# Attention with top-1 routed experts: gate weights, scalings, low parts and a tile's turn in another order

## The chip, the cores and the metric

The kernel runs on one core of a Trainium2 chip. The metric is the device time of one execution in microseconds; the time of a kernel is the median of several runs. The core has a matrix engine (TensorE, PE in the rows), VectorE (DVE), ScalarE (ACT), GpSimd (POOL) and SyncE (SP), which here only issues transfers.

## The reference, cut to what matters

Decayed linear attention over blocks gives `x`; each of its 1536 rows is routed to the one expert with the largest logit, up to a capacity, and scaled with its softmax weight.

```python
# attention: B=2, H=8, S=768, D=64, blocks of 64
intra = einsum('bhij,bhjd->bhid', einsum('bhic,bhjc->bhij', qb, kb) * Dmask, vb)
inter = einsum('bhid,bhde->bhie', qb * lam_pow, kv_state)
out[:, :, sl] = intra + inter
kv_state = lam_block * kv_state + einsum('bhsd,bhse->bhde', kb * rev_pow, vb)
# experts: N=1536, D=512, E=8, F=1024, capacity 384
x = out.transpose(0, 2, 1, 3).reshape(B * S, H * D)
logits = x @ w_gate
expert_idx = argmax(logits, axis=1)
gate_w = softmax(logits)[arange(N), expert_idx]
# the first `capacity` rows of each expert, in order
h = maximum(einsum('ecd,edf->ecf', disp, w1), 0.0)
y = einsum('ecf,efd->ecd', h, w2)
out[i] = gate_w[i] * y[expert_idx[i], pos[i]]
```

## The kernel before, in words

The attention works in chunks of 128 rows, twelve in all (`NTILE`), six for each of the two batches (`NC`). The order of every instruction is written out by hand, and each engine takes its own queue strictly in that order. A chunk passes these steps, spread over several iterations `s` of one loop:

- `load` (L262, SyncE): 512 KB of queries and keys (`qk`) and 512 KB of keys and values (`kv`), four buffers each.
- `decay_q` (L406) and `decay_k` (L417), GpSimd: `qd` and `kd`, scaled with powers of the decay; `kp` (L303, ScalarE) holds those for the keys.
- `score` (L438, TensorE) and `mask` (L448, VectorE), two chunks ahead.
- `state(s)` (L497): the update of the running state on TensorE, added on VectorE (L505, L507) to `tmp`, the old state scaled by ScalarE in `carry` (L485, four instructions).
- `attend(s)` (L464, L471): the chunk's output in PSUM, copied by ScalarE to `xT` (L476).
- `turn(s - 1)` (L520): the output is transposed and multiplied with the gate weights, which lie beside the identity in `iw` (L275, four small transfers issued by ScalarE).
- `gate(s - 1)`: VectorE adds up the logits `l` (L526, L530), finds maximum, index and the one-hot row `oh` (L547); ScalarE copies the row to `xg` (L532, L537) and makes `nm`, `ex` and the sum (L551, L554).
- `place(s - 2)` (L576 to L582): TensorE counts the rows of each expert, VectorE (L583, L587) and GpSimd (L591) make the slot. `scatter` (L608, GpSimd) writes the row into its expert's list in memory; `pad` (L128) writes zeros behind the lists, with the row numbers in `padi`.

The `l` sum, the copy of `xg` (L532) and `oh` read one PSUM bank, `lg`.

Weights come in pieces of 512 KB (L96, four buffers `wraw`). Each is split in a high part `whi` on ScalarE (L103) and a low part `wlo` on VectorE (L111). Pieces 0 to 5 are split within the loop: `HI` puts the high part of piece i at the end of iteration 5 + i, `LO` the low part at the end of iteration 6 + i.

Expert 0 is done in two tiles of 128 rows, `first` and `second` (class `Solo`). `turn` transposes the tile's rows (L192), which SyncE loaded (L161), `rest` makes their low part `xl` (L197), `up` multiplies with one weight piece (L210; after an odd piece ScalarE writes `raw`, L215), `cross` transposes back (L220) and splits into `hh` (L222) and `hl` (L223), `down` multiplies with the second weights (L234). During the attention `first` takes its PSUM banks (`x`, `t`, `h`) in turn from the three buffers that `score` uses. Experts 1 to 7 follow in a loop with 256 rows each (L811, L836); their rows are transposed on VectorE in `shuffle` (L726) and split in `trans` (L736, L737).

Of the kernel before, what the change touches and what calls it, by code (L numbers as in the profile page):

```python
# [18 lines left out]
P = 128  # L19
# [3 lines left out]
E, DFF = 8, 1024  # L23
NT = B * S
NC = S // P
NTILE = NT // P
# [15 lines left out]
def kernel(  # L42
# [71 lines left out]
    def split_w(i):  # L114
        split_hi(i)
        split_lo(i)
# [64 lines left out]
    class Solo:  # L181
# [17 lines left out]

        def up(self, p, between=None):  # L200
            if p % 2 == 0:
# [5 lines left out]
            for n, (a, b, k) in enumerate(terms):  # L207
                if between and n == 2:
                    between()
                nc.tensor.matmul(  # L210
                    ps, lhsT=a[:, P * k:P * k + P], rhs=b[:, k], start=(n == 0), stop=(n == 3 * KD - 1)
                )
# [31 lines left out]
    def attention():  # L244
        with ExitStack() as c2:
# [26 lines left out]
            iw = ac.tile([P, KD, P + E], F32, name="iw")  # L272
            for g in range(2):
                for r in range(2):
                    nc.scalar.dma_start(  # L275
                        out=iw[64 * g:64 * g + 64, r::2, P:P + E], in_=wg[64 * r:64 * r + 64, 2 * g:2 * g + 2]
                    )
            for i in range(1, 4):
# [16 lines left out]
            for a in range(HP):  # L295
# [9 lines left out]
                in_=dt[:, :, :, P - 1:P].rearrange("p r a o -> p a r o"), func=AF.Copy,  # L305
            )

            def busy(n, late=False):
# [169 lines left out]
            def carry(s):  # L478
                c = s % NC
                if c == NC - 1 or c == 0:  # L480
                    return
                old = mem[s % 2]
                tmp[s] = p2.tile([P, HP, D], F32, tag="tmp", name="tmp", bufs=1)
                for a in range(HP):
                    nc.scalar.activation(  # L485
                        out=tmp[s][:, a], in_=old[:, a], func=AF.Copy, scale=qp[:, a, P - 1:P]
                    )
# [34 lines left out]
            def gate(s):  # L522
                if s < 0:
                    return
                l = sm.tile([P, E], F32, tag="l", name="l")
# [8 lines left out]
                )  # L534
                if s == NTILE - 2:
                    first.turn()
                nc.scalar.activation(  # L537
                    out=xg[:, 0:KD - 1],
                    in_=tpp[s][:, :, 0:P].rearrange("p k (g d) -> p k g d", g=2), func=AF.Copy,
                )  # L540
                m8 = sm.tile([P, 8], F32, tag="m8", name="m8")
                nc.vector.max(out=m8, in_=l)
# [64 lines left out]
            def scatter(s):  # L607
# [4 lines left out]
                apart(i, "xs", s >= EARLY)  # L612

            decay_k(0)
            for a in range(HP):
# [9 lines left out]
            load(5, 0)  # L625
            tokens()
            mask(1)
            for s in range(NTILE):
                decay_k(s + 1)
                if s > 0:  # L630
                    state(s, (0, 1, 2, 3))
                attend(s)
                carry(s + 1)
                for k in range(KD):
                    turn(s - 1, k)
                gate(s - 1)
                place(s - 2)
                if s == NTILE - 1:
                    first.rest()
                    for k in range(KD):  # L640
                        turn(s, k)
                    place(s - 1)
# [3 lines left out]
                weight(s - 1)  # L646
                if s in LO:
                    split_lo(LO[s])
                if s in HI:
# [23 lines left out]
            gate(s)  # L673
            first.up(0)
            split_hi(6)
# [27 lines left out]
    def ffn(first):  # L703
        with ExitStack() as c2:
# [62 lines left out]
            second.up(0)  # L767
            shuffle(1, 0)
            shuffle(1, 1)
            second.up(1)  # L770
            split_w(10)
            load_w(14)
            second.up(2)
            second.cross(0)
            split_w(11)
            load_w(15)
# [284 lines left out]
```

## Time and profile before

| | us |
|---|---|
| median of 3 runs | 258.04 (257.35 to 260.33) |
| the profiled execution, its own time | 257.75 |
| its span | 256.0 |
| TensorE busy in it | 237.9 (93%) |
| VectorE, ScalarE, GpSimd busy | 158.0, 132.9, 81.1 |

The span runs from the first to the last instruction; 1.75 us of the profiled time lie outside of it. In rows of a timeline the first number is the start, the second the duration, both in us; the bracket at the end tells how long the engine stood idle before it and what released it. Transposes of the expert rows and the first tile lie between 57 and 93 us, the loop over experts 1 to 7 behind that.

### The profile page before, as it was taken

How to read it: one execution, taken by the hardware profiler on the slowest of the kernel's cores; microseconds unless marked ns; L12 is line 12 of the kernel's file. 1: busy time of each engine (PE TensorE's matmuls, PEld its weight loads, DVE VectorE, ACT ScalarE, POOL GpSimd, SP SyncE). 2: the span in 40 equal slices, each digit the busy share in tenths (PEclk: the TensorE clock that was granted, in tenths of full speed). 3: DMA queues.
4: the chain of work that ended last, by engine and by line, in shares of the span. 5: the costliest groups of instructions: out<-in, count | busy, mean ns of one | idle time of the engine just before them, and what ended most of it. 6: DMA issues, size and time to landing. Idle time of an engine off the chain costs nothing.

```text
span 256.0 us, 5405 instructions
## 1 busy us (share of the span) xinstructions
PE 237.9 (93%) x2071; PEld 211.2 (83%) x2071; DVE 158.0 (62%) x335; ACT 132.9 (52%) x240; POOL 81.1 (32%) x100
## 2 busy tenths in 40 slices
PE   7989999789899899999999999999999999999950
PEld 3778888678778689889989988998998898899850
DVE  4756577788772786792793778479276757912100
ACT  2154556866662685664673656457446546622110
POOL 4583559896585120006004101400500210030130
PEclk9999999999999999999999999999999999999995
DMA  5998899947759869966688497789749698210010
GB/s 131 408 403 301 243 330 386 407 163 249 220 179 276 262 214 316 279 247 250 185 295 264 141 302 237 227 226 308 257 106 319 230 249 242 84 73 3 1 64 3
DMA packets 26894, 58.14 MB, mean 227 GB/s; under 512 B 6377, under 2 KB 13547, under 8 KB 26864
## 3 DMA queue, kind: packets, MB, share of 16 engines
q1 hardware_dynamic: 22752, 50.36, 61.7%
q0 software_dynamic: 3536, 7.37, 7.6%
q8 instruction: 18, 0.29, 0.5%
q10 hardware_dynamic: 576, 0.02, 0.1%
q14 instruction: 12, 0.10, 0.1%
HBM read 50.37 MB, written 11.56 MB: 242 GB/s over the span
## 4 chain that ended last, share of the span: by engine, by line
issue 58%; POOL 15%; PE 10%; DMA 6%; DVE 6%; ACT 1%; POOLq 1%; SPq 0%; DVEq 0%
POOL xs L128 7%; POOL out L175 5%; DMA wraw<-in_wp 4%; PE sc L438 2%; DVE wlo L111 2%; DMA qk<-in_qkv 2%; PE x L464 2%; PE tp L520 2%; PE st L497 1%; PE x L471 1%; DVE pt L448 1%; POOL qd L406 1%; POOL kd L417 1%; POOL out L874 1%; PE solo_ps L210 1%
## 5 line engine op out<-in xcount | busy, mean ns | idle before, releaser
L111 DVE TENSOR_TENSOR wlo<-wraw,whi 128x1024 fp32r<-128x1024 f32 x64 | 77.2, 1216 | 10.9 <-ACT whi L103 8.1
L103 ACT ACTIVATE whi<-wraw 128x1024 fp32r<-128x1024 f32 x64 | 66.6, 1051 | 10.2 <-DMA wraw<-in_wp 10.2
L811 PE MATMUL h<-xh,whi 128*128 128x256 f32 x224 | 61.9, 276 | 0.0
L811 PE MATMUL h<-xl,whi 128*128 128x256 f32 x224 | 61.9, 276 | 0.0
L811 PE MATMUL h<-xh,wlo 128*128 128x256 f32 x224 | 61.9, 276 | 0.0
L175 POOL DMA_INDIRECT out<-y,ti x13 | 13.3, 1025 | 123.7 <-ACT y L844 123.4
L819 DVE SCALAR_TENSOR_TENSOR hl<-h,hh 128x512 fp32r<-128x512 f32 x28 | 19.4, 692 | 40.5 <-ACT hh L818 40.5
L811 PEld LDWEIGHTS h<-xl,whi 128*128 128x128 f32 x224 | 42.1, 188 | 0.3
L811 PEld LDWEIGHTS h<-xh,whi 128*128 128x128 f32 x224 | 42.0, 188 | 0.3
L811 PEld LDWEIGHTS h<-xh,wlo 128*128 128x128 f32 x224 | 42.1, 188 | 0.0
L836 PE MATMUL y<-whi,hl 128*128 128x512 f32 x104 | 41.0, 394 | 0.0
L836 PE MATMUL y<-wlo,hh 128*128 128x512 f32 x104 | 40.8, 392 | 0.0
L836 PE MATMUL y<-whi,hh 128*128 128x512 f32 x104 | 40.4, 388 | 0.0
L818 ACT ACTIVATE hh<-h 128x512 fp32r<-128x512 f32 x28 | 16.8, 598 | 41.0 <-PE h L811 41.0
L836 PEld LDWEIGHTS y<-wlo,hh 128*128 128x128 f32 x104 | 19.5, 188 | 4.3
L836 PEld LDWEIGHTS y<-whi,hh 128*128 128x128 f32 x104 | 19.5, 188 | 4.1
L836 PEld LDWEIGHTS y<-whi,hl 128*128 128x128 f32 x104 | 19.6, 188 | 3.9
L128 POOL DMA_INDIRECT xs<-zero,padi x16 | 18.3, 1142 | 4.9 <-issue 4.6
L476 ACT ACTIVATE xT<-x 128x512 f32<-128x512 f32 x12 | 7.1, 592 | 20.2 <-PE x L471 12.5
L608 POOL DMA_INDIRECT xs<-xg,slot x12 | 15.8, 1313 | 3.7 <-POOL slot L591 1.1
L448 DVE TENSOR_TENSOR pt<-sc,dt 128x512 f32<-128x512 f32 (+1 forms) x26 | 15.6, 643 | 1.9 <-PE sc L438 1.4
L844 ACT ACTIVATE y<-y,wt 128x512 f32<-128x512 f32 x13 | 8.9, 687 | 13.2 <-PE y L836 12.5
(133 smaller groups left out, 355.5 us busy)
## 6 DMA issues: line engine op xcount, KB each, us to landing
wraw<-in_wp SPq DMA_DIRECT2D x64, 512.0 KB
qk<-in_qkv SPq DMA_DIRECT2D x12, 512.0 KB
kv<-in_qkv SPq DMA_DIRECT2D x12, 512.0 KB
rw<-xs SPq DMA_DIRECT2D x28, 128.0 KB
rw<-xs SPq DMA_DIRECT2D x2, 257.0 KB
xs<-zero,padi POOLq DMA_INDIRECT x16
out<-y,ti POOLq DMA_INDIRECT x13
xs<-xg,slot POOLq DMA_INDIRECT x12
```

What stands on the lines that cost most here:

```text
L103: nc.scalar.activation(out=hi, in_=raw[i], func=AF.Copy)
L111: nc.vector.tensor_tensor(out=lo, in0=t, in1=hi.bitcast(F32), op=ALU.subtract)
L128: i = nc.gpsimd.indirect_dma_start(out=xs, out_offset=bass.IndirectOffsetOnAxis(ap=padi[:, e, t:t + 1], axis=0), in_=zero, in_offset=None, ...
L175: i = nc.gpsimd.indirect_dma_start(out=out, out_offset=bass.IndirectOffsetOnAxis(ap=ti[e][:, t:t + 1], axis=0), in_=y, in_offset=None, bou ...
L448: nc.vector.tensor_tensor(out=pt[s][:, r, a], in0=sc[s][r][:, a], in1=dt[:, r, a], op=ALU.mult)
L476: nc.scalar.activation(out=xT[s], in_=x[:, :, 0:2 * P], func=AF.Copy)
L608: i = nc.gpsimd.indirect_dma_start(out=xs, out_offset=bass.IndirectOffsetOnAxis(ap=slot[:, s:s + 1], axis=0), in_=xg_all[:, s], in_offset= ...
L811: nc.tensor.matmul(ps[:, f], lhsT=a[:, k, fs], rhs=b[:, k], start=(n == 0), stop=(n == 3 * KD - 1),)
L818: nc.scalar.activation(out=hh, in_=ps, func=AF.Relu)
L819: nc.vector.scalar_tensor_tensor(out=hl, in0=ps, scalar=0.0, in1=hh.bitcast(F32), op0=ALU.max, op1=ALU.subtract)
L836: nc.tensor.matmul(yp[t], lhsT=a[:, f, tsl], rhs=b[:, f], start=(p == 0 and f == 0 and n == 0), stop=(p == 3 and f == 1 and n == 2),)
L844: nc.scalar.activation(out=y, in_=yp[t], func=AF.Copy, scale=wt[e][:, t, 0:1])
```

## The change

The four transfers of the gate weights are issued behind the copy `kp`. `tokens()`, seven small GpSimd instructions that make row numbers, stands ahead of the first `decay_k`. `carry` of the next chunk is called within `gate`, behind the copies of `xg`, instead of behind `attend`. The low part of a weight piece is made right behind `state` instead of at the end of the same iteration. The first tile's `turn` moves from the gate of chunk 10 to that of chunk 9, its `rest` to the end of iteration 10, and its `up(0)` into iteration 11, with the last chunk's turn after its fifth matmul and the placement of chunk 10 behind it. The two `shuffle` calls of expert 1 move behind `second.cross(0)`.

```diff
--- before.py
+++ after.py
@@ -197,7 +197,7 @@
             nc.vector.tensor_tensor(out=self.xl, in0=self.xp, in1=self.xh.bitcast(F32), op=ALU.subtract)
             tokens_of(0, self.t)
 
-        def up(self, p, between=None):
+        def up(self, p, between=None, at=2):
             if p % 2 == 0:
                 self.hn[p // 2] = self.ps("h")
             ps = self.hn[p // 2][:, 256 * (p % 2):256 * (p % 2) + 256]
@@ -205,7 +205,7 @@
             terms = [(self.xh, w, k) for k in range(KD) for w in (wh, wl)]
             terms += [(self.xl, wh, k) for k in range(KD)]
             for n, (a, b, k) in enumerate(terms):
-                if between and n == 2:
+                if between and n == at:
                     between()
                 nc.tensor.matmul(
                     ps, lhsT=a[:, P * k:P * k + P], rhs=b[:, k], start=(n == 0), stop=(n == 3 * KD - 1)
@@ -270,11 +270,6 @@
             load(0, 0)
             load(0, 1)
             iw = ac.tile([P, KD, P + E], F32, name="iw")
-            for g in range(2):
-                for r in range(2):
-                    nc.scalar.dma_start(
-                        out=iw[64 * g:64 * g + 64, r::2, P:P + E], in_=wg[64 * r:64 * r + 64, 2 * g:2 * g + 2]
-                    )
             for i in range(1, 4):
                 load(i, 0)
                 load(i, 1)
@@ -304,6 +299,11 @@
                 out=kp.rearrange("p (a r) o -> p a r o", r=2),
                 in_=dt[:, :, :, P - 1:P].rearrange("p r a o -> p a r o"), func=AF.Copy,
             )
+            for g in range(2):
+                for r in range(2):
+                    nc.scalar.dma_start(
+                        out=iw[64 * g:64 * g + 64, r::2, P:P + E], in_=wg[64 * r:64 * r + 64, 2 * g:2 * g + 2]
+                    )
 
             def busy(n, late=False):
 
@@ -477,7 +477,7 @@
 
             def carry(s):
                 c = s % NC
-                if c == NC - 1 or c == 0:
+                if c == NC - 1 or c == 0 or s >= NTILE:
                     return
                 old = mem[s % 2]
                 tmp[s] = p2.tile([P, HP, D], F32, tag="tmp", name="tmp", bufs=1)
@@ -521,6 +521,7 @@
 
             def gate(s):
                 if s < 0:
+                    carry(s + 2)
                     return
                 l = sm.tile([P, E], F32, tag="l", name="l")
                 nc.vector.tensor_reduce(
@@ -532,12 +533,13 @@
                 nc.scalar.activation(
                     out=xg[:, KD - 1], in_=lgp[s][:, 0:P].rearrange("p (g d) -> p g d", g=2), func=AF.Copy
                 )
-                if s == NTILE - 2:
-                    first.turn()
                 nc.scalar.activation(
                     out=xg[:, 0:KD - 1],
                     in_=tpp[s][:, :, 0:P].rearrange("p k (g d) -> p k g d", g=2), func=AF.Copy,
                 )
+                if s == NTILE - 3:
+                    first.turn()
+                carry(s + 2)
                 m8 = sm.tile([P, 8], F32, tag="m8", name="m8")
                 nc.vector.max(out=m8, in_=l)
                 i8 = sm.tile([P, 8], U32, tag="i8", name="i8")
@@ -611,6 +613,7 @@
                 )
                 apart(i, "xs", s >= EARLY)
 
+            tokens()
             decay_k(0)
             for a in range(HP):
                 score(0, a)
@@ -623,29 +626,27 @@
             for a in range(HP):
                 score(1, a)
             load(5, 0)
-            tokens()
             mask(1)
             for s in range(NTILE):
                 decay_k(s + 1)
                 if s > 0:
                     state(s, (0, 1, 2, 3))
+                if s in LO:
+                    split_lo(LO[s])
                 attend(s)
-                carry(s + 1)
                 for k in range(KD):
                     turn(s - 1, k)
                 gate(s - 1)
                 place(s - 2)
+                if s == NTILE - 2:
+                    first.rest()
                 if s == NTILE - 1:
-                    first.rest()
-                    for k in range(KD):
-                        turn(s, k)
+                    first.up(0, lambda: [turn(s, k) for k in range(KD)], 5)
                     place(s - 1)
                 for a in range(HP):
                     score(s + 2, a)
                 mask(s + 2)
                 weight(s - 1)
-                if s in LO:
-                    split_lo(LO[s])
                 if s in HI:
                     split_hi(HI[s])
                 load(s + 4, 1)
@@ -671,7 +672,6 @@
                 nc.vector.reduce_max(out=cmax, in_=ct, axis=mybir.AxisListType.X)
 
             gate(s)
-            first.up(0)
             split_hi(6)
             first.up(1, lambda: place(s))
             weight(s)
@@ -765,13 +765,13 @@
             first.finish()
             second.rest()
             second.up(0)
-            shuffle(1, 0)
-            shuffle(1, 1)
             second.up(1)
             split_w(10)
             load_w(14)
             second.up(2)
             second.cross(0)
+            shuffle(1, 0)
+            shuffle(1, 1)
             split_w(11)
             load_w(15)
             second.up(3)
```

## Rows read from the trace of the kernel before

**Rows 1.** The page's first line, then windows: us, each engine's busy time, clock, DMA share, GB/s.

```profile
span 256.0 us, 5405 instructions
...
6.50:93.50 87.00, 79.90 (x1026) 68.94 (x1027) 60.27 (x216) 49.73 (x133) 53.48 (x60) 1.00 0.84 290
93.50:242.00 148.50, 148.50 (x992) 135.69 (x991) 94.51 (x111) 80.64 (x103) 21.53 (x21) 1.00 0.68 213
```

**Rows 2.** TensorE's waits, 6 to 94 us: waited for, us in total, times, longest.

```profile
PE st L497 <- issue: 1.8, 2, 1.1
PE st L497 <- POOL kd L417: 1.3, 2, 1.0
PE solo_ps L234 <- DVE solo_hl L223: 1.0, 1, 1.0
PE st L576 <- DVE mem L507: 0.8, 1, 0.8
...
PE solo_ps L210 <- DVE solo_xl L197: 0.4, 1, 0.4
```

**Rows 3.** Timeline of GpSimd: start, us, engine, line, operation, tiles, count.

```profile
11.38 0.17 POOL L385 IOTA padi<- 128x16 int32 x1
...
13.04 1.04 POOL L417 TENSOR_TENSOR kd<-kv,kp 128x512 f32<-128x512 f32 x1
```

**Rows 4.** Waits of SyncE's queue, 0 to 94 us; timelines of ScalarE and TensorE.

```profile
SPq L262 <- DMA iw<-in_wg: 4.7, 4, 2.1
...
6.50 0.21 ACT L303 ACTIVATE kp<-dt 128x8 f32<-128x8 f32 x1 [1.48 <-DVE dt L297]
...
16.27 0.96 PE L520 MATMUL tp<-iw,xT 128*128 128x136 f32 x6
```

**Rows 5.** Timeline around the gate of chunk 2; brackets: idle before, releaser.

```profile
26.51 1.05 ACT L485 ACTIVATE tmp<-mem,qp 128x64 f32<-128x64 f32 x4
...
27.75 0.17 DVE L547 TENSOR_TENSOR oh<-lg,i 128x8 f16<-128x8 f32 x1 [0.63 <-ACT xg L532]
```

**Rows 6.** Timeline of ScalarE and VectorE around the gate of chunk 6.

```profile
43.19 1.06 ACT L103 ACTIVATE whi<-wraw 128x1024 fp32r<-128x1024 f32 x1 [2.26 <-DMA wraw<-in_wp]
...
45.88 0.17 DVE L547 TENSOR_TENSOR oh<-lg,i 128x8 f16<-128x8 f32 x1 [1.16 <-ACT xg L532]
```

**Rows 7.** Timeline of VectorE and ScalarE, an early iteration and one low part.

```profile
17.27 0.18 DVE L526 TENSOR_REDUCE l<-tp 128x8 f32<-128x24 f32 x1 [1.92 <-PE tp L520]
...
18.83 0.18 ACT L554 ACTIVATION_READ_ACCUMULATOR ex<-l,nm 128x1 f32 x1
...
21.63 0.18 DVE L526 TENSOR_REDUCE l<-tp 128x8 f32<-128x24 f32 x1 [1.17 <-PE tp L520]
...
47.58 1.21 DVE L111 TENSOR_TENSOR wlo<-wraw,whi 128x1024 fp32r<-128x1024 f32 x1
```

**Rows 8.** Timeline around the first tile, and the loads of both tiles' rows.

```profile
57.20 0.33 SPq L161 DMA_DIRECT2D rw<-xs  x1
...
67.81 0.17 PE L576 MATMUL st<-oh,upper 128*128 128x8 f16 x1 [0.66 <-DVE oh L547]
...
68.25 1.04 ACT L103 ACTIVATE whi<-wraw 128x1024 fp32r<-128x1024 f32 x1
...
69.37 0.60 ACT L215 ACTIVATE solo_raw<-solo_ps 128x512 f32<-128x512 f32 x1
...
74.73 0.33 SPq L161 DMA_DIRECT2D rw<-xs  x1
...
78.12 0.63 PE L192 MATMUL solo_ps<-ident,rw 128*128 128x128 f32 x4 [0.24 <-DMA rw<-xs]
```

**Rows 9.** Timeline of VectorE and ScalarE in the second tile.

```profile
84.79 1.30 DVE L726 STREAM_TRANSPOSE xf<-rw 128x512 f32<-128x512 f32 x2
...
85.50 0.60 ACT L222 ACTIVATE solo_hh<-solo_ps 128x512 fp32r<-128x512 f32 x1 [1.05 <-PE solo_ps L220]
...
87.12 0.68 DVE L223 TENSOR_TENSOR solo_hl<-solo_ps,solo_hh 128x512 fp32r<-128x512 f32 x1
```

## The prediction

> **What bounds the kernel now.** I read the windows view first, because it says which stages can give anything at all. From 93.5 to 242 us TensorE is busy 148.50 of 148.50 us [rows 1]. The reader is to see a stage with no hole: whatever happens before 93.5 moves its start, and nothing else in it can be won by reordering the other engines. From 6.5 to 93.5 it is busy 79.90 of 87.00, so it stands still for 7.1 us [rows 1]. All of the change lies there, so 7.1 us is the ceiling of what removed waits can bring. Next I read TensorE's waits in that stretch, which say whom it waits for: `st` for issue or for the decayed keys `kd` (3.1 together), the second tile's `hl` (1.0), the running state `mem` (0.8), the first tile's `xl` (0.4) [rows 2]. No engine is full there; the waits are matters of order in queues that each run strictly in order. So I read the timelines around each wait, and for each moved instruction I ask what now stands behind it.
>
> The sum is made against the profiled execution's own time: span 256.0 [rows 1] and 1.75 around it, 257.75. That is 0.3 below the median of 258.04. All gains below are in us, plus is faster.
>
> **The change part by part.**
>
> *Token numbers first.* The seven small instructions of `tokens()` start at 11.38 and hold GpSimd until `kd` of chunk 1 starts at 13.04: 1.66 us [rows 3]. In their new place GpSimd only waits for the first loads. TensorE's longest wait for `kd` is 1.0 [rows 2], and it is this one. After the move `kd` would start 1.6 sooner, more than the 1.0 that is asked. Gain 1.0; less if the third chunk's load is late next, more if the gap lets the following iteration start early. I keep 0.7 to 1.3.
>
> *Gate weights later.* Their four issues stand first on ScalarE's queue, and SyncE stands still 4.7 us in four waits for them while it has chunk loads to send [rows 4]. Sent behind the `kp` copy of 6.50 [rows 4], they no longer share with the first loads. The bound below is 0 (the later loads pay instead); the bound above is about 0.6, as only the first two loads hold TensorE up. I take 0.4. Behind the four issues on ScalarE nothing is due before the first `xT`. Their first user is the gate of chunk 0, at 16.27 [rows 4], some 1.4 sooner after the change, at 14.9; the deadline has to hold or the part is lost (a rival below).
>
> What speaks against this part stands in the Trainium skill, "DMA: Bandwidth & Descriptors", section "Queues, rings and completion order": each DMA engine takes turns between the queues it has work for, packet by packet. By it the small gate transfers share with the big loads whenever they are sent, and the cost only moves to later loads; this part would bring 0, and the sum would be 0.4 lower. The rows cannot decide it, since SyncE's waits [rows 4] show issues held back and not packets.
>
> Prologue together: 1.0 + 0.4 = **+1.4**.
>
> *State scalings behind the copies.* `oh` waits for ScalarE's `xg` copy, 0.63 at 27.75, because four `tmp` scalings of 1.05 together stand ahead of it [rows 5]. One of the two `st` waits under "issue" (1.8 in two) is the 1.1 of chunk 8, where `oh` waited 1.16 [rows 2, 6]; the rest, 0.7, belongs to this place in the early chunks, and I take **+0.6** there. Price: `tmp` now stands ahead of `nm`, `ex` and the accumulated sum, which come 1.0 later. Two things hang on them: the row weight on VectorE, and `whi` on ScalarE.
>
> *Low parts behind the state update.* Removed with it, in iterations 6 to 10: 1.1 (`st`, chunk 8), 0.8 (`mem`) and the 0.3 that is left of `kd` [rows 2], together 2.2. What is late next: `wlo` of one piece now follows `whi` of that piece directly, and ahead of the gate's `l`. That closes a loop: from `l` to the end of the accumulated sum is 18.83 + 0.18 - 17.27 = 1.74, then `tmp` 1.05 [rows 5], `whi` 1.06 [rows 6], `wlo` 1.21, then the next `l` [rows 7]. The raw sum is 5.06; neighbours on an engine overlap by about 0.1 each, which leaves some 4.76. An iteration without weight work takes 21.63 - 17.27 = 4.36 [rows 7]. So the loop and not TensorE would set the pace, 0.4 more per iteration, and six iterations (6 to 11) have a low part: 6 x 0.4 = 2.4 given back. Bounds: 0 if GpSimd and VectorE have slack enough for the loop not to close (the low part may lie in the shadow of `attend`), 3.0 if neighbours do not overlap. Net **-0.2**, from +2.2 to -0.8.
>
> *First tile a chunk sooner.* Removed: the wait for `xl`, 0.4 [rows 2]. Added: (1) the last but one placement now stands behind the whole of `up(0)`, and the last gate's `l` behind that placement's VectorE work and `weight`. The wait for the last `oh` is 0.66 now [rows 8]. Counted from the end of the last turn, TensorE wants it after the seven matmuls that are left of `up(0)`, the placement and two matmuls, about 1.2; `oh` is there after the placement (1.0), its VectorE work with `weight` (0.7) and the seven small operations from `l` to `oh` (1.1), about 2.8, an estimate from durations near 0.17 [rows 5, 7]. The wait becomes 1.6: -0.9. (2) PSUM's three banks rotate, and one allocation moved: `up(2)` gets the bank of the first hidden half, which is free only when ScalarE's `raw` has read it. `raw` starts at 69.37, behind `whi` at 68.25 (1.04) [rows 8]; `up(2)` follows the gate closely, so about 0.7 of wait is new (0 if the low-part work in front shrinks, 1.1 if all of `whi` counts). (3) The tile's rows are asked for at 57.20; the second tile's took from 74.73 to 78.12, 3.4 us, with TensorE waiting [rows 8]. The turn now falls near 60, so 57.2 + 3.4 = 60.6 may be up to 0.5 late; the rest moves with the same chain, and I take 0. Together **-1.2**, from -2.0 to +0.4.
>
> *Stream transposes behind `cross(0)`.* `hl` starts at 87.12 only because two transposes (1.30) and a low part stood before it; `hh` was done at 85.50 + 0.60 = 86.10 [rows 9]. So `hl` comes 1.0 sooner, and the 1.0 that TensorE waited [rows 2] goes. But the transposes, `wlo` and the expert's `xl` now queue ahead of the second `hl`, which TensorE wants early as well: 86.8 + 1.3 + 1.2 + 0.7 = 90.0, then 0.7 for itself, 90.7, wanted at about 90.2. 0.5 comes back. **+0.5**, from 0 to 1.0.
>
> Sum: 1.4 + 0.6 - 0.2 - 1.2 + 0.5 = +1.1, so 257.75 - 1.1 = 256.65, near **256.7**.
>
> **The rivals.**
>
> *A, removed waits stay removed.* If the low part lies wholly in the shadow of `attend`, the 2.4 of the loop are not paid, and if the bank of `up(2)` is free in time the 0.7 is not either: 1.1 + 2.4 + 0.7 = 4.2 gain, 253.5. For it: VectorE and ScalarE are far from full, 60.27 and 49.73 of 87 [rows 1]. Against it: the loop's five steps are each in the rows, and none of them is optional.
>
> *B, the weight piece lands no sooner (the other side).* Piece 1 makes `whi` wait until 43.19, 2.26 us for its load [rows 6]. So far only its low part waited with it; now that low part stands ahead of the gate of chunk 6. If the piece comes at the same time in spite of an earlier chain, `wlo` ends 43.19 + 1.06 + 1.21 = 45.46, and eight small VectorE operations of about 0.17, such as `l` and `oh` [rows 5, 7], later `st` of chunk 8 can start, at 46.85. Before it started 0.42 behind the `oh` of 45.88 [rows 6], at 46.30. All that was gained until there is lost and 0.55 more; behind it remain +1.1 of waits, -1.2 (three rounds of the loop), -1.2 and +0.5: -1.35, so 259.1. It decides if the piece lands less than about 1.3 sooner than now. Against it: SyncE's issue of the piece hangs on the same chunks, which come sooner.
>
> *C, gate weights late.* If they land after 14.9, TensorE waits in the gate of chunk 0. Issued behind `kp` they have 14.9 - 6.7 = 8 us, in which full chunk loads stand ahead of them; SyncE's longest single wait for them, 2.1 [rows 4], speaks for less. The prologue's 1.4 would go: 258.1.
>
> **How the numbers follow.** Forecast 0.53 (its own range 255.4 to 258.2: the errors of the loop, the bank and the prologue against each other), A 0.20, B 0.11, C 0.09, other 0.07. The range 254.0 to 259.2 takes in B and the nearer half of A and leaves out about 2 in 10. About 1% is what a measurement can tell from no change here: 255.46 and 260.6. Faster needs 2.3 off: A and the low end of the forecast, 0.25. Slower needs B with another mishap, 0.06. The rest, 0.69, lies within 1%.
>
> **What would show it.** Prologue: no wait for `kd` before `st` of chunk 1, SyncE without waits for `iw`, no wait of the first gate matmuls for `iw`. Loop: in iterations 7 to 10 `l` directly behind `wlo`, and `wlo` behind `whi`; the time from one `l` to the next near 4.76. A: it would be 4.4 there and no wait of TensorE. B: `wlo` of piece 1 idle for `whi`, and that for its load, near 43. First tile: `up(2)` waiting for `raw`, and `place` of chunk 11 for `oh` over 1 us. Second tile: no wait at the first `hl`, about 0.5 at the second. The start of expert 1 should move from 93.5 by the sum, to about 92.4. I am wrong if the loop does not close, if the rows or the gate weights are late, or if expert 1 itself gets holes.

## The result, and the profile after

The changed kernel is slower: 261.1 us median of 20 runs against 258.3 of the kernel before in the same comparison, ratio 1.0104 with an interval of 1.0071 to 1.0137. The forecast was 256.7. All ratios leave out executions more than 1.5% above the fastest of their kernel; the profiled one of the changed kernel is such an execution, but later profiles that are not show the same low parts of 2.6 us. The profiled execution of the changed kernel took 263.73, above its own median; its expert loop ran at 22.31 us per expert where another execution of the same kernel ran at 21.89 (first experiment below), so in what follows the two traces are compared by the places that lie ahead of that loop, above all by the start of expert 1 and by the starts of `st`, the state update of a chunk.

The page's first line and the windows view of the kernel after (columns as in [rows 1]):

```profile
span 262.0 us, 5412 instructions
...
6.50:93.50 87.00, 77.93 (x1021) 67.59 (x1022) 62.40 (x213) 49.31 (x133) 48.81 (x53) 1.00 0.82 288
93.50:100.00 6.50, 6.50 (x53) 6.29 (x52) 5.42 (x6) 4.22 (x5) 1.24 (x1) 1.00 0.79 252
```

In the stretch in which TensorE stood still for 7.1 us before [rows 1] it now stands still for 9.1, and behind it there is again no hole. TensorE's waits of the kernel after, 6 to 100 us:

```profile
PE st L497 <- POOL slot L593: 1.9, 1, 1.9
PE st L497 <- issue: 1.6, 1, 1.6
PE st L497 <- POOL kd L417: 1.6, 3, 0.9
PE st L578 <- DVE oh L549: 1.2, 1, 1.2
PE solo_ps L234 <- DVE solo_hl L223: 1.0, 1, 1.0
PE sc L438 <- DMA qk<-in_qkv: 0.7, 1, 0.7
PE solo_ps L192 <- DMA rw<-xs: 0.6, 1, 0.6
PE solo_ps L234 <- ACT solo_hh L222: 0.6, 1, 0.6
```

Against [rows 2] the reader is to see that the waits for `mem` and `xl` are gone as forecast, and that larger ones stand in front of `st`: 1.6 and 1.9 instead of 1.1 and 0.4. Where the time went, by the starts of TensorE's rows in the two timelines:

| place | before | after | gained so far |
|---|---|---|---|
| `st` of chunk 1 | 14.13 | 13.12 | +1.01 |
| `st` of chunk 6 | 36.71 | 35.20 | +1.51 |
| `st` of chunk 8 | 46.30 | 45.62 | +0.68 |
| `st` of chunk 9 | 51.19 | 52.06 | -0.87 |
| `st` of chunk 10 | 56.95 | 57.46 | -0.51 |
| second tile's turn | 78.12 | 78.55 | -0.43 |
| expert 1 | 93.47 | 94.52 | -1.05 |

Two places lose: chunks 7 to 9, over 2 us, and the second tile, 0.6. The first is the larger, and this is its timeline (GpSimd, VectorE and TensorE of the kernel after):

```profile
36.93 1.22 DVE L111 TENSOR_TENSOR wlo<-wraw,whi 128x1024 fp32r<-128x1024 f32 x1
...
37.82 1.23 POOL L417 TENSOR_TENSOR kd<-kv,kp 128x512 f32<-128x512 f32 x1
...
41.05 1.04 POOL L610 DMA_INDIRECT xs<-xg,slot  x1 [0.15 <-POOL qd L406]
...
41.64 2.62 DVE L111 TENSOR_TENSOR wlo<-wraw,whi 128x1024 fp32r<-128x1024 f32 x1 [0.28 <-ACT whi L103]
...
42.12 1.05 POOL L417 TENSOR_TENSOR kd<-kv,kp 128x512 f32<-128x512 f32 x1
...
44.19 0.17 DVE L527 TENSOR_REDUCE l<-tp 128x8 f32<-128x24 f32 x1
...
45.62 0.69 PE L497 MATMUL st<-kv,kd 128*64 128x64 f32 x16 [1.64 <-issue]
...
47.75 2.62 DVE L111 TENSOR_TENSOR wlo<-wraw,whi 128x1024 fp32r<-128x1024 f32 x1 [0.28 <-ACT whi L103]
...
48.23 1.05 POOL L417 TENSOR_TENSOR kd<-kv,kp 128x512 f32<-128x512 f32 x1
```

The low part that took 1.20 to 1.23 in the kernel before (1.21 in [rows 7]) takes 2.62, twice. Both times `kd` lies inside it, at its usual 1.05, and the low part ends 1.09 behind the end of `kd` (42.12 + 1.05 = 43.17, and 41.64 + 2.62 = 44.26). At 36.93 the low part begins 0.89 ahead of `kd`; there it keeps its time and `kd` is the one that grows, to 1.23. The explanation that the experiments test, there called Theory P: a low part and a `kd` don't read at the same time, one stands until the other is done. The Trainium skill, "SBUF — State Buffer", section "Who interferes with whom", has this rule: a VectorE instruction with two inputs in SBUF contends with a GpSimd instruction that reads SBUF, and the one that was issued second stands until the other is done. The trace agrees that it is all or nothing (2.62, with the end 1.09 behind that of `kd`); that the low part, begun 0.48 ahead, was the one to wait is not what the rule says.

### The profile page after: what moved, and what is told of

It is laid out like the page before. It is cut to its first block, busy times and chain, and to the rows that moved or that the text cites. A ratio compares the mean times of both kernels' runs of the same rounds, so it can differ in the third digit from the quotient of the medians.

```text
span 262.0 us, 5412 instructions
## 1 busy us (share of the span) xinstructions
PE 240.1 (92%) x2071; PEld 213.7 (82%) x2071; DVE 161.2 (62%) x335; ACT 133.5 (51%) x240; POOL 77.8 (30%) x100
## 2 busy tenths in 40 slices
DMA packets 26896, 58.15 MB, mean 222 GB/s; under 512 B 6378, under 2 KB 13548, under 8 KB 26865
## 4 chain that ended last, share of the span: by engine, by line
issue 58%; PE 14%; POOL 12%; DVE 6%; DMA 2%; ACT 2%; POOLq 1%; SPq 0%; DVEq 0%
POOL xs L128 6%; POOL out L175 5%; DVE wlo L111 3%; PE x L464 3%; PE sc L438 3%; PE tp L520 3%; DMA kv<-in_qkv 2%; PE x L471 2%; PE st L497 2%; PE solo_ps L210 1%; POOL kd L417 1%; DVE pt L448 1%; ACT whi L103 1%; ACT tmp L485 1%; PE lg L520 1%
## 5 line engine op out<-in xcount | busy, mean ns | idle before, releaser
L111 DVE TENSOR_TENSOR wlo<-wraw,whi 128x1024 fp32r<-128x1024 f32 x64 | 80.1, 1262 | 16.3 <-ACT whi L103 16.3
L811 PE MATMUL h<-xh,wlo 128*128 128x256 f32 x224 | 63.0, 281 | 0.0
L811 PE MATMUL h<-xh,whi 128*128 128x256 f32 x224 | 63.0, 281 | 0.0
L811 PE MATMUL h<-xl,whi 128*128 128x256 f32 x224 | 63.0, 281 | 0.0
L811 PEld LDWEIGHTS h<-xh,wlo 128*128 128x128 f32 x224 | 43.0, 192 | 0.0
L836 PE MATMUL y<-whi,hl 128*128 128x512 f32 x104 | 40.4, 389 | 0.0
L128 POOL DMA_INDIRECT xs<-zero,padi x16 | 16.7, 1044 | 4.9 <-issue 4.3
L438 PE MATMUL sc<-qk 64*128 64x128 f32 x192 | 13.9, 285 | 0.7 <-DMA qk<-in_qkv 0.7
L610 POOL DMA_INDIRECT xs<-xg,slot x12 | 13.3, 1112 | 3.5 <-ACT ex L556 1.2
```

The costliest lines, as they stand in the source:

```text
L111: nc.vector.tensor_tensor(out=lo, in0=t, in1=hi.bitcast(F32), op=ALU.subtract)
L128: i = nc.gpsimd.indirect_dma_start(out=xs, out_offset=bass.IndirectOffsetOnAxis(ap=padi[:, e, t:t + 1], axis=0), in_=zero, in_offset=None, ...
L438: nc.tensor.matmul(sc[s][r][:, a], lhsT=kT[rs, a], rhs=qT[rs, a], start=True, stop=True)
L610: i = nc.gpsimd.indirect_dma_start(out=xs, out_offset=bass.IndirectOffsetOnAxis(ap=slot[:, s:s + 1], axis=0), in_=xg_all[:, s], in_offset= ...
L811: nc.tensor.matmul(ps[:, f], lhsT=a[:, k, fs], rhs=b[:, k], start=(n == 0), stop=(n == 3 * KD - 1),)
L836: nc.tensor.matmul(yp[t], lhsT=a[:, f, tsl], rhs=b[:, f], start=(p == 0 and f == 0 and n == 0), stop=(p == 3 and f == 1 and n == 2),)
```

## The experiments

For a single profile the start of expert 1 says what the attention and the two tiles cost; the ratio says what is left of it over many runs. Two profiles of the changed kernel lie 3.5 us apart in that start (first experiment), so a difference in that column alone shows little; where a wait or a clock makes it, the text names them.

| kernel | ratio to before | `st` of chunk 10 | expert 1 |
|---|---|---|---|
| before | 1 | 56.95 | 93.47 |
| changed | 1.0104 (1.0071 to 1.0137) | 57.46 | 94.52 |
| changed again | 1.0117 (1.0058 to 1.0176) | 57.62 | 97.98 |
| low parts back | 0.9941 (0.9894 to 0.9988) | 55.86 | 93.65 |
| without two `kd` | one run, 258.84 us | 55.08 | 94.14 |
| first tile back | 1.0040 (0.9992 to 1.0087) | 57.68 | 94.79 |
| `kd` ahead of the scatter | 1.0039 (0.9982 to 1.0096) | 55.73 | 92.23 |
| low parts and first tile back | 0.9888 (0.9821 to 0.9955) | 54.43 | 89.63 |
| low parts early in the last two iterations only | 0.9996 (0.9949 to 1.0044) | 54.41 | 92.51 |
| rows ahead of two weight pieces | 1.0264 (1.0191 to 1.0337) | 58.15 | 98.89 |
| `split_lo(6)` written later | 1.0144 (1.0056 to 1.0232) | 58.15 | 95.14 |
| before, with the low parts' move alone | 1.0065 (1.0020 to 1.0110) | 56.72 | 93.65 |
| low parts, first tile and transposes back | 1.0017 (0.9954 to 1.0079) | 54.43 | 93.65 |
| low parts, first tile and gate weights back | one run, 259.25 us | 54.52 | 90.14 |

**The changed kernel once more.** No edit.

> The changed kernel once more, unaltered. In its first profile the expert loop itself was slower: 22.3 us per expert against 21.9, with no hole on TensorE; seven experts make 2.9 us. Theory S, the pace belongs to the single execution: this profile may show 21.9 per expert, and expert 1 starts at 94.0 to 95.0 again. Rival K, the pace belongs to the changed kernel: 22.3 again. Either way low parts 1 and 2 should take 2.6 us again and the ratio to the kernel before lie at 1.006 to 1.014.

The ratio came out as before. Low parts 1 and 2 took 2.62 again. Experts 2 to 6 took 21.89 each, so the pace belongs to the execution, as Theory S has it; a later kernel (gate weights back) showed 22.31 in its single profile. Expert 1, though, began at 97.98, 3.5 later than in the first profile, which no theory had. The two waits of the second tile, and the windows behind them:

```profile
92.24 0.51 PE L234 MATMUL solo_ps<-whi,solo_hh 128*128 128x512 f32 x1 [1.38 <-ACT solo_hh L222]
94.00 0.53 PE L234 MATMUL solo_ps<-whi,solo_hl 128*128 128x512 f32 x1 [1.02 <-DVE solo_hl L223]
```

```profile
87.00:93.00 6.00, 4.54 (x19) 2.79 (x18) 3.53 (x6) 3.42 (x6) 0.00 (x0) 1.00 0.85 282
93.00:99.00 6.00, 5.00 (x19) 4.13 (x20) 4.95 (x6) 3.36 (x6) 0.00 (x0) 0.72 0.71 212
```

Behind 2.4 us of waits the granted clock falls to a mean of 0.72 over six us, so for part of that stretch it is at the lower of its two levels, 1.2 instead of 2.4 GHz. A wait there can thus cost more than its own length. It need not: with 1.6 us of waits in the first profile the clock stayed at 1.00.

**Low parts back.** Where the low part of a piece is made:

```diff
                     state(s, (0, 1, 2, 3))
-                if s in LO:
-                    split_lo(LO[s])
                 attend(s)
...
                 weight(s - 1)
+                if s in LO:
+                    split_lo(LO[s])
```

> The changed kernel with the low parts back at the end of their iteration, all other parts kept. Theory P, the low part in its new place runs at the same time as GpSimd's kd and both cannot have their operands at once: every low part of the attention takes 1.2 again (a scatter beside it 1.8 to 2.0 instead), state of chunk 10 starts about 2.5 sooner than in the changed kernel (near 55), expert 1 near 92.0 to 92.5, time 2 us below the changed kernel. Rival L, the loop of l, scaling, high part and low part alone sets the pace wherever the low part stands: state of chunk 10 gains under 1.

All low parts of the attention took 1.20 to 1.21, and the kernel is faster than the one before by 0.6%, and 1.6 to 1.7% below the changed one. `st` of chunk 10 came only 1.6 sooner, but in this profile the very first `st` came 1.4 late (10.63 against 9.25), so within the attention it is 3.0. Rival L falls. Expert 1 gained 0.9 and not 2: the last placement waited 2.3 for `oh`, because the low part of piece 5 stands ahead of the last gate again while `up(0)` no longer lies between, and the granted clock behind that wait was 0.79 on average from 65 to 73 us.

**Without two `kd`.** The keys of chunks 8 and 9 are left out.

```diff
+                if s in (8, 9):
+                    kd[s] = kd[7]
+                    return
```

> The changed kernel without the two decayed keys of chunks 8 and 9, whose instructions fell into low parts 1 and 2 (left out: the state of these chunks uses the keys of chunk 7). Theory P, low part and kd exclude each other: low parts 1 and 2 take 1.2 instead of 2.6, the next l comes 1.4 sooner each time, and expert 1 starts 2.0 to 2.8 sooner, at 91.7 to 92.5. Rival Q, the scatter ahead of kd or the arriving weights stretch the low part: it still takes 2.0 to 2.6, and expert 1 starts within 1 us of 94.5.

The two low parts, timeline of VectorE in this kernel:

```profile
41.81 1.23 DVE L111 TENSOR_TENSOR wlo<-wraw,whi 128x1024 fp32r<-128x1024 f32 x1 [0.44 <-ACT whi L103]
...
46.53 1.23 DVE L111 TENSOR_TENSOR wlo<-wraw,whi 128x1024 fp32r<-128x1024 f32 x1 [0.28 <-ACT whi L103]
```

With the `kd` gone the low parts take 1.23, although the scatter still stands beside them and weights still arrive: Theory P holds, Rival Q falls. `st` of chunk 10 came 2.4 sooner, as two times 1.4 less what the loop keeps would have it. Expert 1, however, came 0.4 sooner instead of 2.0 to 2.8. Most of the gain is still there at the second tile's last wait: the matmul behind it starts at 90.33 against 92.12 in the changed kernel, 1.8 sooner. From there to expert 1 it takes 3.8 us instead of 2.4, and the clock is what differs (windows of this kernel):

```profile
91.00:94.00 3.00, 3.00 (x9) 2.36 (x8) 3.00 (x4) 1.06 (x1) 0.00 (x0) 0.52 0.71 244
```

The granted clock is 0.52 here, near the lower of the two levels, behind waits of 0.7 and 1.0 in the second tile; in the changed kernel it stayed at 1.00 behind 0.6 and 1.0. These waits are the second loss, and the next runs look for their cause.

**First tile back.** `first.turn()`, `first.rest()` and `first.up(0)` at their old places.

> The changed kernel with the first tile's turn, rest and first up back in their old places. As forecast, the part cost 1.2 (place waiting for oh 1.2 instead of 0.7, up(2) for raw): expert 1 about 1.0 sooner, 93.5. Rival R, this part costs little by itself and the end of this stretch hangs on the rows of expert 1, which come late through scatters and pads on GpSimd: expert 1 within 0.5 of 94.5.

Expert 1 at 94.79, so by the profile Rival R; by the ratio the kernel is 0.6 to 0.8% below the changed one, with intervals that overlap. While the low parts collide, the first tile's move is worth little either way in these profiles.

**`kd` ahead of the scatter.**

```diff
+            decay_k(1)
             for s in range(NTILE):
-                decay_k(s + 1)
...
                 decay_q(s + 2)
+                decay_k(s + 2)
                 if 2 <= s:
                     scatter(s - 2)
```

> The changed kernel with kd of the next chunk issued ahead of the scatter instead of behind it, so that kd (1.05) is over 0.3 us behind the start of the low part. Theory P, low part and kd exclude each other: low parts 1 and 2 take at most 1.6 instead of 2.6, the scatter behind them is stretched to about 2 instead, state of chunk 10 starts about 2.0 to 2.4 sooner than in the changed kernel, near 55.2. Rival Q2, it is the whole of GpSimd's work, scatter included, that holds the low part up: it stays at 2.6. For the end: if the rows of expert 1 bound the start of expert 1, that start gains under 1 us and lies at 93.7 to 94.5; if not, it is near 92.3.

Low parts 1 and 2 took 1.35 and 1.28 (that of piece 0 took 1.75); the scatter behind the first was the one that grew (timelines of GpSimd and VectorE):

```profile
41.34 1.04 POOL L417 TENSOR_TENSOR kd<-kv,kp 128x512 f32<-128x512 f32 x1
...
42.11 1.35 DVE L111 TENSOR_TENSOR wlo<-wraw,whi 128x1024 fp32r<-128x1024 f32 x1 [0.28 <-ACT whi L103]
...
42.54 1.83 POOL L610 DMA_INDIRECT xs<-xg,slot  x1 [0.16 <-POOL kd L417]
```

`kd` was begun first and ended at 42.38; the low part ends 1.08 behind that. The scatter, begun inside the low part, ends 0.91 behind it. Theory P again, now with the order turned, and it says more: a scatter can stand behind a low part too. It need not: the scatter behind low part 2 began 0.02 behind its start and took its usual 1.03. `st` of chunk 10 came 1.7 sooner, a little less than expected. Expert 1 came at 92.23, 2.3 sooner than in the changed kernel: the rows of expert 1, spoken of below, took back little here. The ratio is 1.0039, lower than the changed kernel's with intervals that overlap, and no better than before.

**Low parts and first tile back.** Both edits above together; of the change remain the gate weights, the token numbers, the state scalings and the stream transposes.

> Only the gate weights, token numbers, state scalings and the later stream transposes of the change; the low parts and the first tile's turn in their old places. If the loss sits in these two parts: low parts 1.2 each, state of chunk 10 2 us sooner than in the kernel before (1.4 of the prologue and 0.6 of the scalings), at 55.0, no wait of over 1.0 for oh in the last placement, ratio to the kernel before 0.990 to 0.995. If the first tile's move is a gain by itself and the loss sits in the low parts alone: slower than the kernel with only the low parts put back (0.994).

The best kernel of the study: ratio 0.9888, the whole interval below 1. TensorE's waits, 6 to 100 us, and SyncE's for the zero rows:

```profile
PE st L578 <- DVE mem L507: 0.8, 1, 0.8
PE st L497 <- POOL kd L417: 0.7, 3, 0.3
PE st L578 <- DVE oh L549: 0.7, 1, 0.7
PE sc L438 <- DMA qk<-in_qkv: 0.6, 1, 0.6
PE solo_ps L210 <- DVE solo_xl L197: 0.5, 1, 0.5
PE st L497 <- POOL slot L593: 0.4, 1, 0.4
PE solo_ps L192 <- DMA rw<-xs: 0.3, 1, 0.3
```

```profile
SPq L145 <- DMA xs<-zero,padi: 1.6, 1, 1.6
```

Nothing is over 0.8, and behind its turn the second tile waits for nothing. `xl` and `mem` are waited for again, as in the kernel before, and that costs 1.3; the parts that removed these two waits cost more than that. Against low parts back alone (0.9941) the first tile's move is a loss of about 0.5%, but the two intervals overlap.

**Low parts early in the last two iterations only.**

```diff
-                if s in LO:
+                if s in LO and s >= NTILE - 2:
                     split_lo(LO[s])
```

with the others at the end of their iteration.

> The changed kernel with the low parts behind the state update in the last two iterations alone, where GpSimd makes no kd, and at the end of the iteration before that. Theory P: low parts 1.2 throughout, state of chunk 10 as in the kernel with all low parts put back (about 1.4 sooner than before, 55.5), and the last placement waits for oh 1.2 instead of 2.3, so expert 1 about 1 us sooner than there, near 92.0, ratio 0.988 to 0.993. Rival L, the last chain is not bound by the low part of piece 5: 0.994 as with all of them put back.

The last placement waits 1.2 and not 2.3, as expected, and `st` of chunk 10 is where it should be, 54.41. But expert 1 comes at 92.51 and the ratio is 0.9996, so neither theory's number. The second tile waits 0.7 and 1.0, and SyncE 4.4 for the zero rows, where low parts and first tile back has 0 and 1.6.

**The rows of expert 1.** In the changed kernel the second tile looks like this (timelines of ScalarE, VectorE and TensorE, and SyncE's wait):

```profile
85.13 0.60 ACT L222 ACTIVATE solo_hh<-solo_ps 128x512 fp32r<-128x512 f32 x1 [0.25 <-PE solo_ps L220]
...
86.05 0.69 DVE L223 TENSOR_TENSOR solo_hl<-solo_ps,solo_hh 128x512 fp32r<-128x512 f32 x1
...
88.28 0.17 DVE L169 TENSOR_SCALAR ti<-wt 128x2 int32<-128x2 f32 x1 [1.54 <-DMA wt<-xs]
...
88.45 1.30 DVE L726 STREAM_TRANSPOSE xf<-rw 128x512 f32<-128x512 f32 x2
...
90.37 0.50 PE L234 MATMUL solo_ps<-whi,solo_hh 128*128 128x512 f32 x1 [0.55 <-ACT solo_hh L222]
...
92.12 0.50 PE L234 MATMUL solo_ps<-whi,solo_hl 128*128 128x512 f32 x1 [1.02 <-DVE solo_hl L223]
```

```profile
SPq L145 <- DMA xs<-zero,padi: 4.4, 1, 4.4
```

The first `hl` comes without a wait, against [rows 9]. Behind it VectorE stands for expert 1's rows, until 88.28; in the kernel before it stood too, in the transposes' old place, but only until 84.61 (timeline of VectorE before):

```profile
84.61 0.17 DVE L169 TENSOR_SCALAR ti<-wt 128x2 int32<-128x2 f32 x1 [4.39 <-issue]
```

The profile names no releaser for these 4.39; the instruction reads `wt`, which comes with the rows, so that it was the rows is inferred. They come 3.7 later, with a second tile whose turn is only 0.4 later. SyncE sends for them at 81.43 instead of 77.21, because it holds these transfers back for 4.4 us until the zero rows behind the list of expert 1 have landed. Two experiments were to say why these are late:

```diff
             load_rows(0, 1)
-            load_w(10)
...
-            load_w(11)
             load_rows(1)
+            load_w(10)
+            load_w(11)
```

> The changed kernel with the rows of expert 1 asked for ahead of two weight pieces (10 and 11) instead of behind them. SyncE waited 4.4 to 5.3 us for the zero rows of expert 1 to land, in the shadow of these two pieces. Theory W, the pieces hold the zero rows up: SyncE's wait for them falls under 3 us from the end of the pad, the stream transposes start 2 us sooner and the waits in the second tile (1.6 in the changed kernel) go, so expert 1 starts 1.0 to 2.0 sooner, at 92.5 to 93.5. Rival Z, the zero rows take 4 us by themselves: the wait stays and the pieces only come later, expert 1 at 94.5 or later with waits for weights.

SyncE's wait fell to 3.1, just short of what Theory W says, and its transfers went out 1.6 sooner (79.83 against 81.43). But now the weights were late: the second tile waited 2.0 and 0.6, the granted clock was 0.72 from 87 to 93 and 0.71 from 93 to 99, and expert 1 came at 98.89. The order of rows ahead of weights is no mend. And the low part of piece 6, which began just ahead of the last scatter:

```diff
             count()
-            split_lo(6)
...
             split_hi(7)
+            split_lo(6)
             split_lo(7)
```

> The changed kernel with the low part of piece 6 made behind the high part of piece 7 instead of at once after the counts, where it started 0.04 us ahead of the last scatter and stretched it to 2.0. Theory V, that stretch pushes the pads behind and lets two weight pieces go ahead of the zero rows of expert 1: the last scatter takes 1.0, the pads start 1.0 sooner, SyncE's wait for the zero rows falls from 4.4 to under 3, the waits in the second tile from 1.6 to under 0.6, expert 1 starts about 1.0 to 1.5 sooner, 93.0 to 93.5. Rival X, the pads are late because the loop is late, whatever the scatter takes: the wait stays at 4 or more and expert 1 within 0.5 of 94.5.

This edit doesn't do what it was meant to. Between the two places nothing goes to VectorE, so its queue is the same: the low part of piece 6 still begins right behind the counts, at 71.27, now 0.02 ahead of the last scatter instead of 0.04. The scatter took 0.98 instead of 2.02, and then the first pad behind it 1.96 instead of 0.97. The unaltered kernel had shown the same pair in its second profile (GpSimd, the changed kernel once more; the low part begins at 70.92):

```profile
70.88 0.98 POOL L610 DMA_INDIRECT xs<-xg,slot  x1 [0.28 <-issue]
...
72.17 1.96 POOL L128 DMA_INDIRECT xs<-zero,padi  x1 [0.30 <-issue]
```

SyncE's wait stayed in both, 4.8 and 5.3. Expert 1 came at 95.14, 0.6 later, and as much had arisen ahead of chunk 10 (58.15 against 57.46), where the granted clock was 0.84 from 46 to 57 us. A scatter of its usual length is thus no remedy by itself, as the low part stretches the next GpSimd instruction. A low part that comes later was not tried, Theory V is untested in that form, and why the zero rows land late is open.

**The low parts' move alone, in the kernel before.**

> The kernel before with the low parts behind the state update and nothing else of the change. Theory P: low parts that begin less than half a microsecond ahead of a kd take 2.6, and with tmp still ahead of the copies the same happens to one or two of them; state of chunk 10 0 to 1.5 us later than before (57.0 to 58.5), ratio 1.000 to 1.010. Rival: it is only together with the later scalings that high part, low part and kd meet; then all low parts take 1.2, mem is no longer waited for and state of chunk 10 comes up to 1.5 sooner, ratio 0.993 to 1.000.

Low part 1 took 2.56 at 42.50, with `kd` at 42.91; the others 1.22. `mem` is no longer waited for, but 1.6 of issue and 2.6 of `kd` are. `st` of chunk 10 was 0.2 sooner than before, not later. But 0.7 of that lies ahead of chunk 6 (35.99 against 36.71), where the two kernels are the same; from chunk 6 to chunk 10 the move costs 0.5 (20.73 against 20.24 us). Most of the 0.7 is a wait in front of `st` of chunk 4 that only the kernel before has (its row first, then this kernel's):

```profile
28.18 0.69 PE L497 MATMUL st<-kv,kd 128*64 128x64 f32 x16 [0.62 <-issue]
...
27.46 0.69 PE L497 MATMUL st<-kv,kd 128*64 128x64 f32 x16
```

What remains behind the attention is a wait of 2.6 at the first `hl` of the second tile, where it was 1.0 [rows 2]. Ratio 1.0065, interval above 1: the part loses by itself, without the later scalings.

**The stream transposes back too**, beside low parts and first tile.

> Gate weights, token numbers and state scalings alone; stream transposes in their old place too. As forecast the transposes' move brings 0.5: a wait of about 1.0 at the first hl of the second tile comes back and expert 1 starts 0.5 to 1.0 later than with the move (89.6), at 90.1 to 90.6; ratio 0.990 to 0.994. Rival: the move brings nothing, the second hl takes the wait over: 89.6, ratio 0.989.

Far more than expected: expert 1 at 93.65 instead of 89.63. Timelines of VectorE and TensorE:

```profile
83.45 0.17 DVE L169 TENSOR_SCALAR ti<-wt 128x2 int32<-128x2 f32 x1 [6.21 <-DMA wt<-xs]
...
83.63 1.31 DVE L727 STREAM_TRANSPOSE xf<-rw 128x512 f32<-128x512 f32 x2
...
85.96 0.68 DVE L223 TENSOR_TENSOR solo_hl<-solo_ps,solo_hh 128x512 fp32r<-128x512 f32 x1
...
86.70 0.80 PE L234 MATMUL solo_ps<-whi,solo_hl 128*128 128x512 f32 x1 [3.13 <-DVE solo_hl L223]
```

The transposes wait for the same rows, but in their old place the first `hl` stands behind them. TensorE waits 3.1, and the granted clock from 87 to 93 is 0.78. The difference of 4.0 in the start of expert 1 thus has a wait and a slower clock in it. By the ratio the three parts that are left bring nothing, 1.0017, and with the transposes' move 1.1%. An attention that ends sooner overtakes the rows of expert 1; with the transposes behind `cross(0)` it need not wait for them.

**The gate weights back**, beside low parts and first tile.

> Token numbers, state scalings and the later stream transposes, with the gate weights in their old place ahead of the chunk loads. As forecast the gate weights' move brings 0.4 by itself: state of chunk 1 0.4 later than with it (13.07), near 13.5. Rival, taken from the Trainium skill: small transfers share with the loads wherever they stand, the move brings 0: state of chunk 1 at 13.0 to 13.2, and the first scores not later than 6.7.

`st` of chunk 1 at 13.17 against 13.07: the rival. The move of the gate weights brought 0.1, and the first scores were no later. SyncE's waits for `iw` (4.7 in [rows 4]) were not on the path.

## Why the prediction was wrong, point by point

The sum was +1.1 and the start of expert 1 came 1.05 later. The medians lie 2.8 apart; the 1.7 between the two is placed by no run here, with the start of expert 1 and the pace of its loop changing from execution to execution.

- **Prologue**, +1.4: +1.0 came. The token numbers' 1.0 was right to a tenth against the profile of before (a second profile of the same early code, that of the low parts' move alone, has `st` of chunk 1 at 13.91 and makes it 0.8). The gate weights' 0.4 was not there; the rule of the Trainium skill that was weighed against it ("DMA: Bandwidth & Descriptors", "Queues, rings and completion order") gave 0, and the last run agrees with 0.1, though it shows no packets.
- **State scalings**, +0.6: +0.5 came by chunk 6 (1.01 to 1.51), but it is not shown that the part earned it. The wait that the 0.6 was read from, 0.62 in front of `st` of chunk 4, is absent from the low parts' move alone, where the scalings stand in their old place and the code up to there is that of the kernel before: from `st` of chunk 1 to that of chunk 6 it takes 22.08, as the changed kernel does. The wait belonged to the one profile that was read; no run measures the scalings by themselves.
- **Low parts**, -0.2 with -0.8 as the worst: -2.0 came from chunk 6 to chunk 10. This is the step that failed. The loop that was forecast is there: where no `kd` interferes, `l` follows `l` after 4.72 (56.01 to 60.73), and 4.76 was the estimate. Mis-sized was the term `wlo`, 1.21. That price came from rows where GpSimd had only a scatter beside it, and in the new place it has a `kd`: 2.62 in two of the rounds. The lower bound was mis-worked as well: without overlap of neighbours a round costs 5.06 - 4.36 = 0.7, six rounds 4.2 and not 3.0, which makes the worst -2.0. That this equals what came is a coincidence, since the neighbours did overlap and the loss has another cause. The trace of before held the warning, in GpSimd's timeline: with a low part beside it (42.09, 1.20) a scatter took twice as long as without.

```profile
42.22 1.99 POOL L608 DMA_INDIRECT xs<-xg,slot  x1
...
52.40 1.04 POOL L608 DMA_INDIRECT xs<-xg,slot  x1 [0.16 <-POOL qd L406]
```

  In the old place the low part stretched an instruction for which TensorE hardly waited (0.33 at `st` of chunk 10, for a `kd` behind a stretched pad). In the new one it is itself stretched, with the gate's `l` behind it. The prediction named what is queued behind the moved instruction on its own engine, and did not ask what runs beside it on the other one.
- **First tile**, -1.2: about +0.1 in this profile (from `st` of chunk 10 to the second tile's turn 21.09 against 21.17). The wait for the last `oh` grew to 1.2, where 1.6 was forecast, and `xl` is no longer waited for. The wait of `up(2)` for `raw`, 0.7, exists in none of the profiles, and the rows were in time in the changed kernel. By the ratios of low parts back with and without it the part costs some 0.5%, nearer the forecast than the one profile, but the intervals overlap and its cost is not shown.
- **Stream transposes**, +0.5: the wait at the first `hl` went, but 1.6 came back where 0.5 was forecast, because VectorE stood 1.5 for expert 1's rows. The reading of [rows 9] was at fault: `hl` started at 87.12 not only because two transposes and a low part stood before it, but because VectorE had stood idle for 4.39 in front of these transposes. The sum then took the rows as there at 86.8; they came at 88.28. In a kernel whose attention ends sooner the same part is worth 4.0 in single profiles, with the clock's share in it, and 1.3% by the ratios. The rows were the term that was missing: their lateness was priced for the first tile only.

Rival B was right in the sign and nearest in size (259.1 against 261.1), with another mechanism: `whi` of piece 1 did not wait for its load at 40.57, the piece was there. Rivals A and C did not come to be: TensorE stood still longer than before, and never for `iw`.

## What to carry to other kernels

Before a VectorE instruction with two SBUF inputs is moved, look at what GpSimd does in the new place: its duration in the old place holds only for what ran beside it there. A removed wait can come back at the next thing that arrives by itself, here a list's rows; look for the transfer that a faster stage will overtake, and put what waits for it behind what does not. Read a wait that is to carry a price in a second profile of the same code, as the one of the scalings was in one profile only. When a change has several parts, measure them apart: four of these together bring 1.1%, and the other two take that back and as much again.

## What the runs showed of the hardware

- A low part (VectorE, 128x1024, two inputs in SBUF) and a `kd` (GpSimd, 128x512) don't overlap: the one takes 2.62 instead of 1.22 or the other 1.23 to 1.41 instead of 1.05. A low part that had `kd` 0.4 to 0.5 behind its start ended 1.09 after the end of `kd` as if it had not begun; with `kd` 0.7 to 0.9 behind it kept its time. Why a start of 0.48 did not count is not settled.
- A scatter that begins 0.04 us or more behind the start of a low part ends some 0.9 behind the low part's end (42.22 + 1.99 = 44.21 against 42.09 + 1.20 = 43.29 in the kernel before): 1.8 to 2.0 instead of 1.0 where it begins within 0.3 of that start. Two that began 0.02 behind kept their 1.0, and the low part took 1.28.
- TensorE's granted clock fell behind waits of 1.8 to 3.6 us in all in six profiles, to means of 0.71 to 0.84 over 6 to 11 us, and stayed at 1.00 behind a wait of 2.6 in another (the low parts' move alone). Behind the same two waits in front of `st`, 1.6 and 1.9, it fell to 0.84 from 46 to 57 us in two profiles (rows ahead of two weight pieces, `split_lo(6)` written later) and stayed at 1.00 in three. What decides it these runs don't show.
- The expert loop, without a hole on TensorE, took 21.89 per expert in most executions and 22.31 in two, with kernels whose loops are the same.
